# Attention on 64-token halves, with the running state carried twice per chunk, in a fused gated-linear-attention and MLP kernel

## The chip, the cores and the metric

The kernel runs on one core of one Trainium2 chip. A core has five engines that run side by side, each with its own instruction queue: PE (TensorE, matrix products), DVE (VectorE), ACT (ScalarE), POOL (GpSimd) and SP (SyncE, which here only starts transfers). Data lies in HBM; transfers (DMAs) bring it to the on-chip memory SBUF; products land in a second memory, PSUM, which has eight banks. The metric is the device time in microseconds of one execution; lower is better. A profile is one more execution, recorded instruction by instruction; its span runs from the first to the last instruction.

## The reference

Gated linear attention comes first, for 4 batches, 8 heads, 768 tokens and 48 values per head. Its output, with the heads side by side (384 values per token), goes through a normalisation and a two-layer MLP, and is added to the MLP's result:

```python
for t in range(S):
    state = alpha[:, :, t, :, None] * state + k[:, :, t] (outer) v[:, :, t]
    y[:, :, t] = q[:, :, t] @ state
x  = y as (batch, token, 384)
xn = (x - mean) / sqrt(var + 1e-6) * g_ln
out = x + relu(xn @ w_ch1) @ w_ch2          # 384 -> 1536 -> 384
```

All of it is in float32; the two weight matrices arrive as float64 and are rounded on the chip.

## The kernel before

**Attention.** The 768 tokens are six chunks of 128 (`c`); with four batches (`b`) there are 24 blocks of attention, `attention(c, b)`. A block takes the logarithm of alpha, sums it along the chunk with a product with a triangular matrix (`lps`, L249), and takes two exponentials: `eq` (the product of the alphas up to each token) and `ek` (its inverse). Then q is scaled by `eq` and k by `ek`, and the recurrence turns into plain matrix products:

- both are transposed on PE (`tps`, L272) and copied to SBUF (`qkT`, L276 on ScalarE, L278 on VectorE);
- scores are k times q for each head (`aps`, L285). Heads lie in pairs `p`, of which head `i` sits on rows 0 to 47 or 64 to 111. `copy_predicated` (L289) writes what lies on or under the diagonal into a score tile `at`. There are two of these tiles in all, taken by turns; their other halves stay zero;
- outputs are scores times v (L307) plus q times the state at the start of the chunk (L302), added up in one PSUM tile `yps`. Chunk 0 has no state, so no L302;
- the state's update is k times v over the chunk (`sps`, L321), added to the state by VectorE (L326) and multiplied by the chunk's total gate by GpSimd (L331). The gate is the last row of `eq`, turned from a row into a column by two small transfers through HBM (`row`, L262, and `gate`, L294). The last chunk updates no state.

The output `x` is copied out of PSUM (L311), sent to HBM as `kept` for the final addition, normalised, and transposed (`xps`, L349) into `xT` for the MLP.

**The MLP.** In chunk 0 it is plain: `hidden` (L372, 36 products over 12 column blocks) and `project` (L384, 48 products). In the later chunks both layers use a scheme with fewer products and more additions: `hidden_product` (L612) and `product` (L455), with sums on VectorE (`combine_x`, `combine_hidden`) and GpSimd (`combine_first`, `combine_weights`, which rework the weights once). The weights come in 12 pieces of 768 KB, six of the first matrix and then six of the second. Three stage buffers hold pieces in flight. `round_weights` takes three operations on VectorE (L168, L170, L172), one on ScalarE (L174), and further ones on VectorE (L176 to L183).

**What sets the order.** Every part of the work is a Python generator that yields after each step, and the string `ORDER` says which generator takes its next step: a lower-case letter is a block of attention (a to x, in the order of chunk and batch), A to L a weight piece, M the MLP's products, N, S, X their sums, R the activations, O the fetching of `kept`. A letter whose generator has ended does nothing. Each engine gets its instructions in the order in which the steps issue them and keeps that order; a semaphore holds an instruction until its operands are there and its target is free. All input transfers go through SP's queue, at the start alpha, then k and q, then v for the four batches, then three weight pieces. `attention` loads the alpha, k and q of a later block at its sixth step and the v of the next chunk near its end. The pool `ps` has two PSUM banks under the tag `s` (outputs, state update, `xps`), three under `a` (prefix sums, transposes, scores) and three under `m` (MLP).

Of the kernel before, what the change touches and what calls it, by code (L numbers as in the profile page):

```python
# [9 lines left out]
FP32 = mybir.dt.float32  # L10
# [15 lines left out]
    "babdabcdcabadcbacabbdabaabacababdabacbdbccbadAccdddcBcCedfeacbacaeBeffcgbaededbe"  # L26
    "eghfbAefgfcachfbdcheaaffbaefgdjBddeedbdcgfbeicCjgdfihcgjdCeAhccAgBDfghddEfeOgegi"
    "DfDeeiMfhMMMiMDMMiegMGEgEMMMOfeGghhigMMjhiCEfggFMhOGFHFgMGghMiHkfMMfiHeFIjhfHeMM"
    "IkJSIhhkhhlMMjIMfMglKJKjJLfgMljjLKLhhMSSMihSikMhOSgiMMSSMgShjkSjhiiMXjiSXSiXiXMk"
    "kMXkSllMXMXMlSMMXnMnMMkSMSMSiXmMSXMnMSMSMSMSjkMMkikjMXlMMMMMMRMllMMMljOMRSMMMSlk"  # L30
    "jlklMjjSRimMMnMSMjRMMMnMMMMkMnnmnMMMkMRMpjMMMnMRlMlllnmMmiRmOlMSmMRmMoMmmOMMJMRM"
    "SmSjmNSjlRMMRmoNinjkkNMmNMMkolMNRpoMlOKpMNMmMMMoMmoNmMNkNMMMNMMNMnMNqMkMNMMMopMM"
    "NSMMnolMoMlNpkNMoMMMOkOMMonnXXXXpMMXXMMXXXpoMMMMMMMMpXMMXMMoMMMrMMMMqMMMrMMMmnMM"
    "pRMomRnprmmMRqRopMMpMRMoMMmRmMMMMMrprnMnrnMMMoopppnMtpMqRMMMOMtrqMqnMMoMpqMprMRq"
    "RMMqNsMqMOMNRMNtrRnrMNMqMqqNMssRMMMNssoMMMNMNNMNsMMMNopMqqqqqrMMNMMsNtpMMNMMOprM"
    "MMNqsMqtMMooMMsNpMMXMMsMXXMstMqrrXtuXXXMtMMXXMMvMMMMXsvMMMtXMstMOrMMMMMMMMMvMMrr"
    "rsMtMvOsMMrtMMMMLuRMsMMvvMMMMMRRMtMrRMuMORvxMMMRRMstrMMstRqttsMqRuMsMMNRMuMRNMMN"
    "NMvMtuurvMxMMMMNsNtRtMMwNNvMMMsrMNMwMMNNMNMMwtNMMuMMuuMMMMMNuMwMNMMNwMMuttsxMMuv"
    "XXXvxMvuuXXXXxvwxMXMxxMMuwMXMwxMMXMMXMMMMMvMMwMwMxMMMRMuOwMuOMMwMMMMwuMMxwMwRMRM"
    "MxRMMRMvMMMMwxMMMMMMMMMuMMuMRMRRvMMMRNwxuRMMvMOMRxMMxvwMMNwMxNNMNxRNMMuxMMwMNMvM"  # L40
    "MONMwMNNMNMMMNwMMNMxMxMMvMMxwNMONMMNxMMMvMMXvOXXXMXXXMMMMMMXXMMMMMMMMXMMMMMRMXMM"
    "RMMMMMMMMMMMMMMMRRMMMMORMMMMMRMMMMRMMMMMMMMMRMRRMRMMNMMMNMMMNNNRMMNNMNMNMMMNNMMM"
    "ONMNMMMMMMMMMMMMMNNMMNMMMMMMM"
# [4 lines left out]
def kernel(  # L48
# [59 lines left out]

    r = np.arange(P)
    upto = (r[None, :] >= r[:, None]).astype(np.float32)  # L110
# [4 lines left out]
    def load(c, b, names="akqv"):  # L115
        for n, src in (("a", alpha), ("k", k), ("q", q), ("v", v)):
            if n not in names:
                continue
            t = raw.tile([P, H, D], FP32, name=f"r{n}", tag=f"r{n}",
                         bufs=B)  # L120
            nc.sync.dma_start(t, src[b, c * P:(c + 1) * P])
            raws[n, c, b] = t

# [88 lines left out]
    sts = [cpool.tile([P, NP, 2, D], FP32, name=f"st{b}") for b in range(B)]  # L212
    for b in range(B):
        nc.vector.memset(eqs[b].rearrange("p a b c -> p (a b) c")[:, :, D:], 0.0)
        nc.vector.memset(qks[b].rearrange("p i a b c -> p (i a b) c")[:, :, D:], 0.0)
        nc.gpsimd.memset(sts[b], 0.0)

# [7 lines left out]
    def eq_of(c, b):  # L225
        return eqs[b if c < 2 else b % 2]

    def qk_of(c, b):
        return qks[b if c < 2 else b % 3]


    ats = [cpool.tile([P, 2, NP, P], FP32, name=f"at{i}") for i in range(2)]
# [9 lines left out]
    def attention(c, b):  # L242
# [16 lines left out]
        if c + 1 < NCB:  # L259
            row = dram.tile([1, NP, P], FP32, name="row", tag="row")  # L260
            gate = work.tile([P, NP], FP32, name="gate", tag="gate", bufs=B)
            nc.sync.dma_start(row, eq_of(c, b)[P - 1:P].rearrange("o a b c -> o a (b c)"))  # L262
# [5 lines left out]
        qkT = work.tile([R, 2, NP, P], FP32, name="qkT", tag="qkT", bufs=2)  # L268
        for i in range(2):
            tps = ps.tile([R, NP, P], FP32, name="tps", tag="a", bufs=3)  # L270
            for p in range(NP):
                nc.tensor.transpose(  # L272
                    tps[:, p], qk_of(c, b)[:, i, p].rearrange("p a b -> p (a b)")[:, :R], ident)
            yield
            if i == 0 or c < 2:
                nc.scalar.copy(out=qkT[:, i], in_=tps)  # L276
            else:
                nc.vector.tensor_copy(out=qkT[:, i], in_=tps)  # L278
            yield
        at = ats[b % len(ats)]  # L280
        aps = [ps.tile([P, NP, P], FP32, name=f"aps{i}", tag="a", bufs=3) for i in range(2)]
        for p in range(NP):
            for i in range(2):
                rows = slice(64 * i, 64 * i + D)
                nc.tensor.matmul(aps[i][:, p], qkT[rows, 1, p], qkT[rows, 0, p],  # L285
                                 start=True, stop=True)
        yield
        for i in range(2):
            nc.vector.copy_predicated(out=at[:, i], data=aps[i],  # L289
                                      mask=mask.unsqueeze(1).broadcast_to([P, NP, P]))  # L290
        yield
        if c + 1 < NCB:
            with nc.allow_non_contiguous_dma(reason="one row to columns"):
                nc.sync.dma_start(gate, row.rearrange("o a c -> c (o a)"))  # L294
        yield
        vt = raws.pop(("v", c, b))
        yps = ps.tile([P, NP, 2, D], FP32, name="yps", tag="s")
        sides = [slice(64 * s, 64 * s + 64) for s in range(2)]
        for p in range(NP):
            if c > 0:  # L300
                for s in sides:
                    nc.tensor.matmul(yps[s, p].rearrange("p a b -> p (a b)"), qkT[:, 0, p, s],  # L302
                                     sts[b][:R, p].rearrange("p a b -> p (a b)"),
                                     start=True, stop=False)
            for i in range(2):
                for s in sides:
                    nc.tensor.matmul(yps[s, p, i], at[:, i, p, s], vt[:, 2 * p + i],  # L307
                                     start=(c == 0), stop=(c == 0 or i == 1))
# [6 lines left out]
        yield  # L315
        if c + 1 < NCB:
            sps = ps.tile([R, NP, D], FP32, name="sps", tag="s")
            heads = list(enumerate((slice(0, 64), slice(64, R))))
            for p in range(NP):
                for i, s in heads:  # L320
                    nc.tensor.matmul(sps[s, p], qk_of(c, b)[:, 1, p, i, :s.stop - s.start],  # L321
                                     vt[:, 2 * p + i], start=True, stop=True)
        yield
        if c + 1 < NCB:
            for i, s in heads:
                nc.vector.tensor_add(sts[b][s, :, i], sps[s], sts[b][s, :, i])  # L326
        yield
        if c + 1 < NCB:
            load(c + 1, b, "v")
            st = sts[b].rearrange("p a b d -> p a (b d)")  # L330
            nc.gpsimd.tensor_mul(st, st, gate.unsqueeze(2).broadcast_to([P, NP, 2 * D]))  # L331
# [393 lines left out]
```

## Time and profile before

| What | Value |
|---|---|
| Median of three runs | 476.33 us (474.06 to 476.4) |
| Span of the profiled execution | 472.3 us |
| PE busy | 457.1 us (97% of the span), 3,690 records |
| VectorE, ScalarE, GpSimd busy | 356.6, 152.9, 222.7 us |
| Outputs: scores x v (L307), q x state (L302) | 768 and 320 records, 36.5 and 29.8 us busy |
| Scores (L285) | 384 records, 28.6 us busy |
| Bytes moved | 43.29 MB in 40,132 packets |

The page gives the span of the profiled execution and no separate time for it; the median of the runs is 4.0 us above that span, which stands for what lies around it. A float32 product shows as two PE records. Busy times of PE count a record from its start to its end, and records overlap, so the distance of successive starts says more about a product's price than its length. "Idle before" names what ended a wait.

### The profile page before, as it was taken

What the parts mean: (1) busy time and instruction counts of PE and PEld (TensorE: products, weight loads), DVE (VectorE), ACT (ScalarE), POOL (GpSimd) and SP (SyncE); (2) the same over time, 40 slices, a digit from 0 to 9 for tenths busy, and PEclk for the clock granted to TensorE, in tenths of its full rate; (3) what the DMA queues carried; (4) which work ended last, traced back from release to release, by engine and by line L of the source; (5) the groups of instructions that cost most, each with busy time, mean ns of one, the idle gap of its engine ahead of it and who ended that gap; (6) DMA issues with size and microseconds to landing.
All of it is one profiled execution on the core that took longest, in us unless ns stands there. A gap on an engine that the chain in (4) does not pass through costs nothing.

```text
span 472.3 us, 9365 instructions
## 1 busy us (share of the span) xinstructions
PE 457.1 (97%) x3690; PEld 384.5 (81%) x3690; DVE 356.6 (76%) x662; ACT 152.9 (32%) x335; POOL 222.7 (47%) x222
## 2 busy tenths in 40 slices
PE   7899999999999999999999999999999999998996
PEld 5768465567688889998898998898998899987896
DVE  3799899867377799876788867688677579765673
ACT  4576354511033523124342121543031341223300
POOL 4142103069969990727461426460435360544513
PEclk9999999999999999999999999999999999999999
DMA  8986856403301422240331231330020110210001
GB/s 260 334 248 196 282 157 224 123 19 102 85 17 52 129 75 67 70 118 15 104 101 52 86 102 51 83 101 1 34 81 23 35 35 0 80 56 0 1 18 51
DMA packets 40132, 43.29 MB, mean 92 GB/s; under 512 B 13956, under 2 KB 36228, under 8 KB 40088
## 3 DMA queue, kind: packets, MB, share of 16 engines
q1 hardware_dynamic: 39544, 42.56, 29.4%
q8 instruction: 29, 0.48, 0.4%
q10 hardware_dynamic: 544, 0.13, 0.1%
q14 instruction: 15, 0.12, 0.1%
HBM read 33.20 MB, written 9.48 MB: 90 GB/s over the span
## 4 chain that ended last, share of the span: by engine, by line
PE 85%; DVE 5%; POOL 4%; ACT 2%; DMA 2%; issue 2%; POOLq 0%; DVEq 0%; ACTq 0%
PE ops L455 24%; PE hps L612 24%; PE hps L372 7%; PE ops L384 7%; PE aps L285 5%; PE yps L307 4%; PE tps L272 4%; PE yps L302 4%; PE lps L249 3%; PE sps L321 2%; PE xps L349 2%; DMA rk<-in_k_dram 1%; DVE at L289 1%; DVE sum L588 1%; DMA ra<-in_alpha_dram 1%
## 5 line engine op out<-in xcount | busy, mean ns | idle before, releaser
L471 POOL TENSOR_TENSOR ob<-ob,u 128x192 f32<-128x192 f32 x40 | 27.5, 699 | 83.3 <-DVE ob L468 63.9
L612 PE MATMUL hps<-sum,w 128*128 128x256 f32 x240 | 59.9, 382 | 1.1 <-DVE hT L655 1.1
L612 PEld LDWEIGHTS hps<-sum,w 128*128 128x128 f32 x240 | 44.7, 190 | 7.9 <-DVE hT L655 1.5
L455 PE MATMUL ops<-w,hT 128*128 128x192 f32 x280 | 49.6, 328 | 0.0
L664 ACT ACTIVATE hT<-hT 128x512 f32<-128x512 f32 x60 | 36.3, 628 | 35.6 <-POOL hT L634 21.3
L455 PEld LDWEIGHTS ops<-w,hT 128*128 128x128 f32 x280 | 45.7, 190 | 1.1
L331 POOL TENSOR_TENSOR st<-st,gate 128x384 f32<-128x384 f32 x20 | 19.1, 959 | 53.6 <-DVE st L326 44.3
L631 POOL TENSOR_TENSOR hT<-hT,u 128x512 f32<-128x512 f32 x10 | 12.9, 1287 | 56.9 <-DVE u L630 56.9
L256 POOL TENSOR_TENSOR qk<-rk,ek 128x384 f32<-128x384 f32 x22 | 23.3, 1059 | 30.0 <-PE sps L321 12.6
L307 PE MATMUL yps<-rv,at 128*64 128x48 f32 x768 | 36.5, 219 | 0.1
L289 DVE COPY_PREDICATED at<-consts,aps 128x512 f32<-128x512 int32 x48 | 32.2, 724 | 3.6 <-PE aps L285 3.2
L307 PEld LDWEIGHTS yps<-rv,at 128*64 128x64 f32 x768 | 32.9, 138 | 0.6 <-DVE at L289 0.3
L372 PE MATMUL hps<-xT,w 128*128 128x512 f32 x72 | 32.4, 597 | 0.0
L384 PE MATMUL ops<-w,hT 128*128 128x384 f32 x96 | 32.2, 488 | 0.0
L612 PE MATMUL hps<-xT,w 128*128 128x256 f32 x120 | 31.1, 382 | 0.9 <-DVE hT L644 0.9
L285 PE MATMUL aps<-qkT 48*128 48x128 f32 x384 | 28.6, 285 | 2.1 <-DVE at L289 1.3
L285 PEld LDWEIGHTS aps<-qkT 48*128 48x128 f32 x384 | 23.8, 187 | 8.0 <-issue 4.0
L302 PE MATMUL yps<-st,qkT 112*64 112x96 f32 x320 | 29.8, 257 | 0.0
L455 PE MATMUL ops<-ws,sum 128*128 128x192 f32 x160 | 28.9, 328 | 0.7 <-DVE sum L442 0.7
L455 PE MATMUL ops<-ws,hT 128*128 128x192 f32 x160 | 29.5, 327 | 0.0
L276 ACT COPY qkT<-tps 112x512 f32<-112x512 f32 x32 | 18.2, 597 | 29.0 <-PE tps L272 25.7
L455 PEld LDWEIGHTS ops<-ws,sum 128*128 128x128 f32 x160 | 26.3, 190 | 1.4 <-DVE sum L442 1.0
(141 smaller groups left out, 1020.9 us busy)
## 6 DMA issues: line engine op xcount, KB each, us to landing
ws<-in_moe_w_ch_dram SPq DMA_DIRECT2D x12, 768.0 KB, 6.1
ra<-in_alpha_dram SPq DMA_DIRECT2D x24, 192.0 KB, 2.6
rk<-in_k_dram SPq DMA_DIRECT2D x24, 192.0 KB, 3.4
rq<-in_q_dram SPq DMA_DIRECT2D x24, 192.0 KB
rv<-in_v_dram SPq DMA_DIRECT2D x24, 192.0 KB, 2.8
kept<-x SPq DMA_DIRECT2D x24, 192.0 KB, 1.9
ob<-kept SPq DMA_DIRECT2D x24, 192.0 KB, 2.9
out_dram<-ob SPq DMA_DIRECT2D x19, 192.0 KB, 1.9
```

What stands on the lines that cost most here:

```text
L256: nc.gpsimd.tensor_mul(qk[:, 1, :, :D], raws.pop(("k", c, b)), ek)
L285: nc.tensor.matmul(aps[i][:, p], qkT[rows, 1, p], qkT[rows, 0, p], start=True, stop=True)
L289: nc.vector.copy_predicated(out=at[:, i], data=aps[i], mask=mask.unsqueeze(1).broadcast_to([P, NP, P]))
L302: nc.tensor.matmul(yps[s, p].rearrange("p a b -> p (a b)"), qkT[:, 0, p, s], sts[b][:R, p].rearrange("p a b -> p (a b)"), start=True, stop ...
L307: nc.tensor.matmul(yps[s, p, i], at[:, i, p, s], vt[:, 2 * p + i], start=(c == 0), stop=(c == 0 or i == 1))
L331: nc.gpsimd.tensor_mul(st, st, gate.unsqueeze(2).broadcast_to([P, NP, 2 * D]))
L372: nc.tensor.matmul(hps, w1[:, f, j * P:(j + 1) * P], xT_of[c][:, f], start=(f == 0), stop=(f == NF - 1))
L384: nc.tensor.matmul(ops_of[b], hT_of[c][:, j, b], w2[:, j], start=(j == 0), stop=(j == NJ - 1))
L455: nc.tensor.matmul(acc, lhs[:, j], rhs[:, j], start=(j == 0), stop=(j == NT - 1))
L471: getattr(nc.gpsimd, f"tensor_{op}")(x, x, y)
L612: nc.tensor.matmul(acc[:, i], w, b, start=True, stop=True)
L664: nc.scalar.activation(out=x, in_=x, func=AFT.Relu)
```

## The change

Each chunk of 128 tokens is now worked on as two halves of 64.

- The triangular matrix is cut into two blocks, so that the sums of logarithms start anew at token 64, and `eq` and `ek` refer to the start of the half. There are two gates per chunk (two rows of `eq`, two columns), also in the last chunk.
- The transposed q is no longer in a tile of its own: it is copied straight into the score tile `at`, head 0 of a pair into rows 0 to 63 and head 1 into rows 64 to 111. The scores of a head go to the other half of the rows of the same tile. Scores are thus 16 products of 64x64 per block instead of 8 of 128x128, and each half's column of `at` holds q on some rows and scores on the others.
- v is loaded twice, in two layouts: `rv` has the rows that the state's update reads where v lies in its own half, and `va` has v in the rows that face the scores, while its other rows take the state. One product over all rows of `at` and `va` then gives scores x v plus q x state. A v load is six transfers of 64 rows with pieces of 48 values (192 bytes); it was one transfer with rows of 1,536 bytes.
- The state is updated after each half: `ups` holds two updates per chunk (one in the last), each is added by VectorE and multiplied by its gate by GpSimd, and after each a `carry` copies the state, head by head, into `va`: of this chunk for the second half, of the next chunk for its first half. Both copies of a carry are on ScalarE. Chunk 0 goes the same way, with a state that a memset has zeroed.
- All copies out of the transposes are on ScalarE (L298, L300 of the new kernel); the VectorE copy is gone.
- The state tile has half the width; `ORDER` is another string throughout.

The core of the diff, in which `HS` is 64 and `halves` are the two half ranges of 128 rows:

```diff
-    upto = (r[None, :] >= r[:, None]).astype(np.float32)
+    upto = ((r[None, :] >= r[:, None]) & (r[None, :] // HS == r[:, None] // HS)).astype(np.float32)
...
+            rv = raw.tile([P, NP, D], FP32, name="rv", tag="rv", bufs=B)
+            va = raw.tile([P, 2, NP, 2, D], FP32, name="va", tag="va", bufs=B)
+            src = v[b, c * P:(c + 1) * P].rearrange("(s t) (p i) d -> i s t p d", s=2, i=2)
+            for i in range(2):
+                nc.sync.dma_start(rv[halves[i]], src[i, i])
+                for s in range(2):
+                    nc.sync.dma_start(va[halves[1 - i], s, :, i], src[i, s])
...
-    ats = [cpool.tile([P, 2, NP, P], FP32, name=f"at{i}") for i in range(2)]
+    ats = [cpool.tile([P, NP, 2, 2, HS], FP32, name=f"at{i}") for i in range(2)]
...
-            if i == 0 or c < 2:
-                nc.scalar.copy(out=qkT[:, i], in_=tps)
+            if i == 0:
+                for j in range(2):
+                    nc.scalar.copy(out=at[rows[j], :, j], in_=tv[rows[j]])
             else:
-                nc.vector.tensor_copy(out=qkT[:, i], in_=tps)
+                nc.scalar.copy(out=kT, in_=tv)
...
+        for p in range(NP):
+            for s in range(2):
+                for i in range(2):
+                    rs = slice(64 * i, 64 * i + D)
+                    nc.tensor.matmul(aps[i][halves[1 - i], p, s], kT[rs, p, s], at[rs, p, i, s],
+                                     start=True, stop=True)
...
+        for p in range(NP):
+            for s, up in enumerate(ups):
+                for i, h in enumerate(heads):
+                    vs = rv[halves[s], p] if s == i else va[halves[s], s, p, i]
+                    nc.tensor.matmul(up[h, p], qk_of(c, b)[halves[s], 1, p, i, :h.stop - h.start],
+                                     vs, start=True, stop=True)
...
+        def carry(s, to):
+            for i, h in enumerate(heads):
+                nc.scalar.copy(out=to[h, s, :, i], in_=st[h])
+
+        for s, up in enumerate(ups):
+            nc.vector.tensor_add(st, up, st)
+            yield
+            nc.gpsimd.tensor_mul(st, st, gate[:R, s].unsqueeze(2).broadcast_to([R, NP, D]))
+            yield
+            if s == 0:
+                carry(1, va)
+                yield
...
         for p in range(NP):
             for i in range(2):
-                rows = slice(64 * i, 64 * i + D)
...
+                rs = slice(0, P if i == 0 else R)
+                for s in range(2):
+                    nc.tensor.matmul(yps[halves[s], p, i], at[rs, p, i, s], va[rs, s, p, i],
+                                     start=True, stop=True)
+        yield
+        if not last:
+            load(c + 1, b, "v")
+        yield
+        if not last:
+            carry(0, raws["v", c + 1, b][1])
```

## The prediction, made before the changed kernel ran

> **What bounds the kernel now.** I read the page's first part, then the busy times by stretch, then the start: its DMA queue, its VectorE and its PE timelines.
>
> ```profile
> span 472.3 us, 9365 instructions
> PE 457.1 (97%) x3690; PEld 384.5 (81%) x3690; DVE 356.6 (76%) x662; ACT 152.9 (32%) x335; POOL 222.7 (47%) x222
> ...
> PE 85%; DVE 5%; POOL 4%; ACT 2%; DMA 2%; issue 2%; POOLq 0%; DVEq 0%; ACTq 0%
> ```
>
> PE is busy 97% of the span and carries 85% of the chain that ended last: what PE has to do, and when it can begin, is the time. The stretches (busy us of each engine) say where it does not:
>
> ```profile
> 0.00:20.00 20.00, 15.22 (x143) 12.01 (x144) 9.94 (x21) 8.25 (x17) 8.07 (x15) 1.00 0.91 305
> 20.00:40.00 20.00, 18.29 (x269) 14.06 (x268) 18.79 (x38) 14.70 (x34) 6.58 (x7) 1.00 0.78 219
> 60.00:80.00 20.00, 20.00 (x145) 11.05 (x143) 19.36 (x32) 9.21 (x17) 4.72 (x5) 1.00 0.55 172
> ```
>
> PE's idle time is in the first 40 us (8.5 of some 15 us in all). From 20 to 40 us ScalarE (fourth number) is the fullest that it ever is, VectorE (third) is nearly full from 20 to 100, and the DMA share is 0.91 and 0.78. So the start is a chain of several engines, and everything after it is PE. The queue on SP at the start (start, us, what):
>
> ```profile
> 7.49 1.85 SPq L121 DMA_DIRECT2D rv<-in_v_dram  x4
> 9.58 1.88 SPq L156 DMA_DIRECT2D ws<-in_moe_w_ch_dram  x3
> ...
> 13.34 0.59 SPq L121 DMA_DIRECT2D rq<-in_q_dram  x1
> 16.11 0.33 SPq L121 DMA_DIRECT2D ra<-in_alpha_dram  x1
> 18.17 0.33 SPq L121 DMA_DIRECT2D rk<-in_k_dram  x1
> 20.21 0.33 SPq L121 DMA_DIRECT2D rq<-in_q_dram  x1
> ```
>
> An issue costs 0.46 us of the queue (1.85/4). In the built program each load waits for the load eight places ahead to have landed; the starts at 16.11, 18.17 and 20.21 are that wait for the three weight pieces, which so landed at 16, 18 and 20 us. VectorE begins to round the first piece at 18.3 and needs 2.43 us for the three operations:
>
> ```profile
> 18.30 0.94 DVE L168 TENSOR_SCALAR w<-ws 128x768 int32<-128x768 int32 x1
> 19.27 0.96 DVE L170 SCALAR_TENSOR_TENSOR w<-ws,w 128x768 f32<-128x768 uint32 x1
> 20.26 0.56 DVE L172 TENSOR_SCALAR ws<-ws 128x768 int32<-128x768 int32 x1
> 20.73 0.94 DVE L168 TENSOR_SCALAR w<-ws 128x768 int32<-128x768 int32 x1
> ```
>
> Last, PE where attention runs without a gap; successive starts give the price of each block:
>
> ```profile
> 44.78 0.35 PE L302 MATMUL yps<-st,qkT 112*64 112x96 f32 x4
> 44.97 0.39 PE L307 MATMUL yps<-rv,at 128*64 128x48 f32 x8
> 45.19 0.35 PE L302 MATMUL yps<-st,qkT 112*64 112x96 f32 x4
> 45.37 0.39 PE L307 MATMUL yps<-rv,at 128*64 128x48 f32 x8
> 45.59 0.63 PE L321 MATMUL sps<-rv,qk 128*64 128x48 f32 x16
> 46.15 1.16 PE L285 MATMUL aps<-qkT 48*128 48x128 f32 x16
> 47.24 1.12 PE L372 MATMUL hps<-xT,w 128*128 128x512 f32 x2
> ```
>
> A float32 matmul is two records. Outputs with the state cost 4 x (0.19 + 0.22) = 1.64 us, the update of the state 0.56, the scores 1.09. Single starts in the trace alternate: 6 and 105 ns in the scores, 6 and 40 to 52 ns where 48 columns meet 64 columns of weights. So a matmul's second record waits for its first, and the next matmul, on another part of the array, starts beside that second record. The price is one pass plus 6 ns per matmul, whatever the number of free parts.
>
> **What the Trainium skill says.** "TensorE: Matmul & The Clock Gate", Part 3, has matmuls on different tiles of the array overlap but start in order: the 6 ns agree. Its section LDWEIGHTS prices a weight load at columns/1.2 ns: 107 for 128 columns, 53 for 64, close to the 105 and 52 here, so 64 columns of weights set the pass whether 48 or 64 columns stream. The same page, Part 1 (engine queue depths), says that ScalarE and VectorE are strictly first in, first out; every order in this trace agrees, and the argument rests on it. "DMA: Bandwidth & Descriptors", Specifications, wants pieces of 512 B for line rate; the new v loads move 192 B pieces, and no run here shows such a piece.
>
> **The change part by part. PE after the change.**
> - Scores: 16 matmuls of 64x64 instead of 8 of 128 columns: 16 x (53+6 ns) = 0.95, plus the 0.15 to 0.2 that a block of scores has over its matmuls now (1.09 - 8 x 0.111): 1.1 us, as before. 24 times: 0.
> - State update: 16 matmuls (8 in the last chunk) instead of 8: 16 x 0.055 + 0.1 = 1.0 instead of 0.56; 20 x 0.44, and 4 x 0.56 where there was none: +11 us.
> - Outputs: 16 matmuls, 0.22 x 4 + 0.07 = 0.95, instead of 1.64: 20 x -0.69 = -14 us.
> Sum -3 us. Bounds: if four free parts let the update run at half its price, -13; if changing between tile shapes costs 0.1 us more per block, +4.
>
> **Other engines.** ScalarE: per block of attention two copies of q and one of k (0.60 each, the qkT copy's row) instead of one or two, and four small carries of some 0.3 (the 128x192 copies): +1.8 us in the first two chunks, where both were already on it. VectorE: 16 copies of 0.68 go (-11 us), all after chunk 1. GpSimd: 44 products of half size, 0.65 estimated from 0.96, instead of 20: +9 us. All three have room after 100 us (ScalarE 6 to 17 of 40), none in the start.
>
> **The queue and the start, followed through the order that was built.** Each v load is six issues instead of one: 24 issues instead of 4 ahead of the weights. From 7.5 us, with the wait for eight places ahead until the last q has landed (some 11 us), then 16 x 0.43: the weights are issued at 18.2 to 19, not 9.6, and land at 22.2, 24.3, 26.3 (2.05 us each as now), not 16 to 20. Behind them on SP: rows and gates (the first gate waits for weight piece 2 by the eight-places rule: issued 24.4, there at 27.5) and the loads of chunk 1.
> What is late next. In the new order ScalarE has two weight steps ahead of the first logarithm of chunk 1; they wait for VectorE's rounding of pieces 1 and 2. VectorE: 22.3 + 2.43, 24.7 + 2.3 = 27.0; ScalarE 27.1 + 1.0 = 28.1, logarithm to 28.6, PE's first prefix matmul of chunk 1 at 28.8, where it is 25.4 now. PE's list before it (two score blocks, one update) is over at some 19.4: PE idles 9 us.
> Then the outputs of batch 0: they wait for update, add, gate product, carry, as the state now comes in as rows of the second operand even in chunk 0. From 28 us ScalarE has, until x of the last batch: 5 logarithms (2.6), 8 exponentials (3.9), one weight step (1.0), 8 q and 3 k copies (6.6), 16 carries (4.8), 4 x (1.9), 2 rstd pairs (1.0): 21.9 us, in one queue with waits for PE (the two score tiles also hold q and are free only after the outputs). I get some 3 us of such waits, so 53; then norm, transpose, copy, 2.5: the first hidden product can start at 55.5, against 47.2 now. Bounds: 52 with no wait at all; 58 if 192 B pieces are slow (0.64 us a load) or PE's clock falls back in the gap: the first filler matmuls took 0.21 us per record where warm transposes of the same size take 0.11.
>
> **The sum.** I count what either PE list holds from the first hidden product on, at the prices above and 0.86, 0.65, 0.43, 0.33 us for the four product kinds (two issue distances each): 408.6 us before, 409 after, since the new order leaves about as much attention behind that point. Before, 472.3 - 47.2 - 408.6 = 16.5 us of small waits and tail; I keep them, as nothing in this order removes them. After: 55.5 + 409 + 16.5 = 481. Before's median 476.33 is 4.0 above the span: 485.
> VectorE's last rounding, which held the projections (PE reaches the last third at 101.4, VectorE ends at 97.8), has the same sum of work up to there (82 and 81 us) and a later start; it ends near 106, while PE needs it at 111. It is covered by the same delay; if PE started earlier, it would bind near 104.
>
> **The rivals.**
> - The state's round trip stalls PE in every chunk: update, add, product, carry, add, product, carry is some 4 us with hand-overs, more behind GpSimd's 1.3 us operations. For it: 24 such trips. Against: PE's new order has 4 to 10 us of products between update and outputs. If 20 of them wait 0.5 us: +10, 495.
> - Faster: the start is no longer than now. For it: PE is short of other work only there, and the list up to the first hidden product is some 4 us shorter. It needs the first hidden product by 47 us; then -3 us of PE gives about 473. The point that decides is 50 us. Against: two engines in strict order behind weights that are issued 9 us later.
> - Half of the delay returns, for instance because later waits, 16.5 us now, shrink when other engines have run ahead: 477, no difference.
> - The change does not do what it says: PE's work does not fall, as the doubled update eats the gain. This I hold for nearly true; it is in the sum.
>
> **How the numbers follow.** My case (480 to 491) 0.58; round trips 0.14; no difference 0.13; faster 0.15. Half a per cent is about what a measurement of this kernel can tell. Range 474 to 494: it takes in the start at 52 to 58 (481.5 to 487.5) with PE's -13 to +4, and part of the round trips and of the faster case. Faster 0.15, same 0.13, slower 0.72.
>
> **What would show it.** The first hidden product at 53 to 58 us; weights issued near 18 us; a PE gap of 7 to 10 us before 30 us; ScalarE over 90% busy from 28 to 53; 4,138 PE records (3,690 + 384 scores - 320 state products + 384 updates); update 1.0, scores 1.1, outputs 0.95 us per block; the time from the first hidden product to the end within 5 us of the 425 now. Wrong would be a first hidden product before 50 us, or update blocks of 0.6.

## The result, and the profile after

The kernel after takes 516.08 us (median of four, 514.23 to 516.55), the kernel before 476.37 beside it: a ratio of 1.0833, 95% interval 1.0802 to 1.0863, 40 us slower. The profiled execution of after has a span of 514.5 us. The page's first part and chain:

```profile
span 514.5 us, 10644 instructions
PE 459.2 (89%) x4138; PEld 379.2 (74%) x4138; DVE 365.2 (71%) x650; ACT 208.6 (41%) x463; POOL 236.5 (46%) x254
...
PE 62%; DVE 15%; DMA 6%; SPq 5%; POOL 4%; ACT 4%; issue 3%; POOLq 0%; DVEq 0%
```

PE's busy time is what it was (459.2 for 457.1 us). Its idle time is not: 55.3 us for 15.2. In the sum, the loss is PE standing still; the equal busy times hide less work and slower matmuls, as shown below. PE's share of the chain fell from 85 to 62%; VectorE, transfers and SP's queue took its place. The stretches say when (same columns as before: PE, weight loads, VectorE, ScalarE, GpSimd, granted clock, DMA share, GB/s):

```profile
0.00:20.00 20.00, 12.51 (x74) 9.22 (x74) 6.13 (x16) 9.64 (x19) 8.73 (x23) 0.91 0.63 168
20.00:40.00 20.00, 6.54 (x116) 4.49 (x118) 12.39 (x19) 6.48 (x12) 1.62 (x3) 0.66 0.81 235
60.00:80.00 20.00, 14.57 (x101) 8.61 (x100) 14.30 (x26) 9.33 (x21) 1.46 (x2) 0.85 0.67 167
```

From 20 to 40 us no computing engine is even two thirds busy: each waits for another. PE is still a quarter idle from 60 to 80, where it was full. Places in PE's order, read from the trace (us at which the first record of each kind starts):

| | before | after |
|---|---|---|
| first hidden product (chunk 0) | 47.2 | 65.8 |
| first projection of chunk 0 | 89.0 | 114.4 |
| first product of chunk 1 | 126.9 | 167.2 |
| from there to the span's end | 345.4 | 347.3 |

So 18.6 us are lost up to the first hidden product, another 21.7 up to the first product of chunk 1, and 1.9 in the remaining 347. SP's queue at the start, as shown of before:

```profile
7.19 0.67 SPq L136 DMA_DIRECT2D rv<-in_v_dram  x1
7.90 1.25 SPq L138 DMA_DIRECT2D va<-in_v_dram  x2
...
23.46 1.66 SPq L173 DMA_DIRECT2D ws<-in_moe_w_ch_dram  x3
...
32.10 0.39 SPq L317 DMA_DIRECT2D gate<-row  x1
```

A v issue costs 0.61 to 0.67 us; 24 of them, with hardly a wait between, put the weights at 23.5 us (9.6 before) and the first gate at 32.1 (21.2 before). VectorE begins to round at 28.09 (18.30 before). PE's wait in the start, and its blocks where they stand next to each other:

```profile
34.61 1.65 PE L268 MATMUL lps<-la,consts 128*128 128x384 f32 x2 [12.68 <-ACT la L265]
...
39.64 1.14 PE L349 MATMUL yps<-va,at 128*64 128x48 f32 x32 [0.45 <-DVE st L337]
40.71 0.65 PE L292 MATMUL tps<-consts,more 128*112 128x128 f32 x4
...
46.82 1.15 PE L307 MATMUL aps<-at,kT 48*64 48x64 f32 x32
47.90 1.87 PE L268 MATMUL lps<-la,consts 128*128 128x384 f32 x4
...
81.87 0.25 PE L327 MATMUL ups<-rv,qk 64*64 64x48 f32 x1
...
82.48 0.70 PE L403 MATMUL hps<-xT,w 128*128 128x512 f32 x1
```

PE waits 12.7 us for the first logarithm of chunk 1. Outputs cost 1.07 us (40.71 - 39.64; 1.64 before), scores 1.08, the doubled update 0.61 (82.48 - 81.87; 0.56 before, for half as many matmuls). So PE's work did fall, by some 8 us as an estimate: 20 x 0.57 = 11 us in the outputs, less 20 x 0.05 in the updates and less four new updates of some 0.5 us in the last chunk. None of it shows in the busy time, because the matmuls lasted longer: in the run without the state's trip, below, the same 4,138 records are busy for 448.7 us at a mean granted clock of 0.984; in after they take 459.2 us at 0.966.

Last, pieces of the chain of after between the v issues and the first hidden product (start, us, what):

```profile
46.35 2.23 DMA gate<-row
...
52.09 2.52 DMA gate<-row
54.74 0.52 POOL st L339
...
57.35 2.35 DVE w L200 x3
```

The chain runs through the state's trip (gate transfer, gate product, carry, add), and through rounding that stands between the trip's steps in VectorE's queue.

### The profile page after: what moved, and what is told of

It reads as the page before. It is cut to its first block, busy times and chain, and to the rows that moved or that the text cites. A ratio compares the mean times of both kernels' runs of the same rounds, so it can differ in the third digit from the quotient of the medians.

```text
span 514.5 us, 10644 instructions
## 1 busy us (share of the span) xinstructions
PE 459.2 (89%) x4138; PEld 379.2 (74%) x4138; DVE 365.2 (71%) x650; ACT 208.6 (41%) x463; POOL 236.5 (46%) x254
## 4 chain that ended last, share of the span: by engine, by line
PE 62%; DVE 15%; DMA 6%; SPq 5%; POOL 4%; ACT 4%; issue 3%; POOLq 0%; DVEq 0%
PE hps L643 22%; PE ops L486 22%; PE yps L349 3%; PE ops L415 3%; SPq L138 3%; PE aps L307 3%; PE tps L292 3%; DMA gate<-row 2%; PE lps L268 2%; DVE w L187 2%; DVE ws L193 2%; PE ups L327 2%; DVE w L185 2%; DVE w L196 2%; DMA ws<-in_moe_w_ch_dram 2%
## 5 line engine op out<-in xcount | busy, mean ns | idle before, releaser
L339 POOL TENSOR_TENSOR st<-st,gate 112x192 f32<-112x192 f32 x44 | 30.5, 697 | 125.3 <-DVE st L337 69.6
L334 ACT COPY va<-st 64x192 f32<-64x192 f32 x88 | 30.7, 349 | 54.8 <-POOL st L339 45.1
L312 DVE COPY_PREDICATED at<-consts,aps 64x512 f32<-64x512 int32 x48 | 35.1, 732 | 15.0 <-PE aps L307 13.7
L268 PE MATMUL lps<-la,consts 128*128 128x384 f32 x48 | 23.4, 576 | 21.5 <-ACT la L265 21.4
L298 ACT COPY at<-tps 64x512 f32<-64x512 f32 (+1 forms) x48 | 27.8, 579 | 22.7 <-PE tps L292 22.1
L307 PEld LDWEIGHTS aps<-at,kT 48*64 48x64 f32 x768 | 24.9, 137 | 11.3 <-ACT kT L300 5.4
L307 PE MATMUL aps<-at,kT 48*64 48x64 f32 x768 | 28.3, 225 | 3.9 <-ACT kT L300 3.8
L349 PEld LDWEIGHTS yps<-va,at 128*64 128x64 f32 (+1 forms) x768 | 23.7, 137 | 8.1 <-DVE st L337 4.6
L292 PE MATMUL tps<-consts,qk 128*112 128x128 f32 x176 | 26.9, 288 | 3.0 <-DVE qk L277 1.6
L349 PE MATMUL yps<-va,at 128*64 128x48 f32 (+1 forms) x768 | 25.7, 223 | 4.0 <-DVE st L337 4.0
```

Of the source, the lines that this page charges most:

```text
L268: nc.tensor.matmul(lps[:, :DM], tri, la, start=True, stop=True)
L292: nc.tensor.transpose(tps[:, p], qk_of(c, b)[:, i, p].rearrange("p a b -> p (a b)")[:, :R], ident)
L307: nc.tensor.matmul(aps[i][halves[1 - i], p, s], kT[rs, p, s], at[rs, p, i, s], start=True, stop=True)
L312: nc.vector.copy_predicated(out=at[h, :, i], data=aps[i][h], mask=mask[h, h].unsqueeze(1).unsqueeze(1).broadcast_to([HS, NP, 2, HS]))
L334: nc.scalar.copy(out=to[h, s, :, i], in_=st[h])
L339: nc.gpsimd.tensor_mul(st, st, gate[:R, s].unsqueeze(2).broadcast_to([R, NP, D]))
```

## The experiments

Theories: A, the six v issues of a block hold up SP's queue. B, GpSimd's sums of weights run beside VectorE's rounding, and the two slow each other. C, the state's trip delays PE, by PE's own waits (C1) or by its operations on the other engines (C2). O, the new sequence is at fault. Where an edit builds on another, it says so. Ratios are to the kernel before in the same session; its medians lay between 474.0 and 476.4 us, so a difference of medians between two sessions is uncertain by some 2 us.

### A: the v issues

Weights ahead of v, in after:

```
-    for names in ("a", "kq", "v"):
+    for names in ("a", "kq"):
...
     for i in range(STAGED):
         load_weights(i)
+    for b in range(B):
+        load(0, b, "v")
```

> The kernel after, with one edit: the 24 issues of the first v loads stand behind the first three weight pieces in SP's queue instead of ahead of them. Nothing is left out. Theory A (the six v issues per block hold up SP's one queue, at the start and later): the weights are issued near 10 us instead of 23.5, VectorE rounds from about 16 us instead of 28.1, but 15 us of v issues now stand ahead of rows, gates and the loads of chunk 1, so only part of the 13 us returns: first hidden product at 55 to 60 us instead of 65.8, total 506 to 511. Theory B (VectorE and GpSimd slow each other from 116 to 165 us in the new order): the late part is unchanged, 510 to 516. Theory C (PE waits for update, add, gate product and carry): the same start gain, at most, 508 to 516.

Measured: 518.05 us, ratio 1.0909 (1.0857 to 1.0961), first hidden product at 68.7. Nothing is gained: the rounding begins at 23.0 instead of 28.1, behind the masking and the first add in VectorE's queue, but the first gates are issued at 34.2 and 36.2, 2 us later than in after.

Two issues of whole rows, in after (called V below):

```
-            rv = raw.tile([P, NP, D], FP32, name="rv", tag="rv", bufs=B)
...
-            for i in range(2):
-                nc.sync.dma_start(rv[halves[i]], src[i, i])
-                for s in range(2):
-                    nc.sync.dma_start(va[halves[1 - i], s, :, i], src[i, s])
+            for h in halves:
+                nc.sync.dma_start(va[h].rearrange("t s p i d -> t s (p i d)"), src)
...
+        carry(0, va)
         for s, up in enumerate(ups):
```

> The kernel after, with v loaded by two issues of 64 rows x 2 x 1,536 B per block instead of six of 64 x 4 x 192 B; a row then also fills the place of the state of the first half, so this carry moves from the end of the block before to after the update. Nothing is left out. Theory A: an issue stays near 0.5 us, so 4 us of queue per chunk instead of 15.7; weights issued near 12 us, first hidden product at 52 to 56 us, gates no longer 5 us late, total 483 to 495. Theory B: the start's 10 to 12 us return, the other 21 us of loss between the first hidden product and the first product of chunk 1 stay: 502 to 507. Theory C: as B, or worse since the carry now stands between update and add: 503 to 512.

Measured: 512.43 us, ratio 1.0779 (1.0734 to 1.0825).

```profile
7.33 5.28 SPq L135 DMA_DIRECT2D va<-in_v_dram  x8
12.65 1.89 SPq L170 DMA_DIRECT2D ws<-in_moe_w_ch_dram  x3
```

Weights are issued at 12.65, VectorE rounds from 21.5, and still the first hidden product starts at 64.0. A alone is refuted as the cause of the 40 us.

Both edits:

> The kernel after with both edits: v by two issues per block, and those of chunk 0 behind the first three weight pieces. Nothing is left out. Theory A: weights issued near 8 to 9 us, VectorE rounds from 15 us, first hidden product at 48 to 52 us, total 478 to 490. Theory B and C: the start's 14 to 17 us return and nothing else: 499 to 503.

Measured: 514.91 us, 1.0815 (1.0760 to 1.0869), first hidden product at 66.2. With v by two issues, too, weights ahead of v bring nothing.

The kernel before with six v issues (the core of the edit):

```
...
+                for i in range(2):
+                    nc.sync.dma_start(more_v[halves[i]], src[i, i])
+                    for h in range(2):
+                        nc.sync.dma_start(to[halves[h], :, i], src[i, h])
...
```

> The kernel before, whose v loads are each made of six issues of 64 x 4 x 192 B: four that fill the same tile, two that fill a tile that nothing reads. Nothing else is changed and nothing is left out. Theory A: 0.65 us an issue, 15.7 us of queue per chunk, weights issued near 23 us; the first hidden product moves from 47 to 60 to 66 us and the total from 476 to between 493 and 512. Theory B and C (the loss is of the new order or of the state's trip): the start's delay alone, as far as it isn't made up later: 480 to 492.

Measured: 498.25 us, 1.0485 (1.0436 to 1.0534), first hidden product at 61.2. SP's queue in it:

```profile
7.11 0.65 SPq L126 DMA_DIRECT2D rw<-in_v_dram  x1
7.80 1.25 SPq L128 DMA_DIRECT2D rv<-in_v_dram  x2
...
23.49 1.66 SPq L168 DMA_DIRECT2D ws<-in_moe_w_ch_dram  x3
```

The issues alone cost the kernel before 22 us, yet going from six to two in after returns 4 (and the intervals of after and of V, 1.0802 to 1.0863 and 1.0734 to 1.0825, overlap). Something as long lies beside the issues.

### O: the sequence

V in the old order, step by step (each letter of a batch in the old string stands for these steps of the new blocks):

```
masking    -> masking, gate, update, add, product, carry, add, product
outputs    -> outputs, x
transposes -> transposes of x, their copy
```

> The kernel after with v by two issues per block, and its steps put back into the order of the kernel before: each step of attention stands where the old order has its counterpart; the update, the two adds, gate products and carries follow the masking of the scores at once; x follows the outputs, and the transposed x its transposes, at once. Nothing is left out. Theory O (the sequence that was searched anew makes the start serial: in it ScalarE has two weight steps ahead of the logarithms of chunk 1, and few products stand beside attention): first hidden product at 46 to 54 us, first product of chunk 1 at 127 to 138, total 472 to 488. Theory C (the state's trip itself costs it, in any order): PE waits at every block, first hidden product after 58 us, total 500 or more. Theory B (VectorE and GpSimd slow each other): in the old order the rounding is over before the sums begin, so as O.

Measured: 562.04 us, 1.1807 (1.1737 to 1.1877), first hidden product at 84.7. One thing changes here in what is computed: the tile with the queries of chunk 2's last batch is written again before its outputs are formed, so these take another block's queries, at the same work. O is refuted in this form: set out in this way, the old sequence is 50 us slower than the new one.

V with the logarithms of chunk 1 ahead of the weight steps (the stretch of the string that changes):

```
-bbbbaaABAdaBAeecacfeCCafdfAdbb
+bbbbaaefeeffABAdaBAcacCCadAdbb
```

> The kernel after with v by two issues per block, and six letters of its order moved: logarithm, prefix product and exponentials of the first two batches of chunk 1 stand ahead of the first weight steps instead of behind them. Nothing is left out. Against 512.4 us with v by two issues alone. Theory O: PE's gap of 7.8 us before 28 us closes, the prefix products run near 20 us, first hidden product at 55 to 59 us instead of 64.0, total 503 to 508. Theory C: the outputs of chunk 0 still wait for add, gate product and carry, which are behind the rounding on VectorE: first hidden product at 61 to 64 us, total 509 to 513. Theory B: no change after 64 us, so at most the start's gain.

Measured: 515.30 us, 1.0849 (1.0805 to 1.0893), first hidden product at 67.0. PE's gap shrinks from 7.8 to 4.9 us, and a wait of 5.7 us for an add comes behind it.

V with the weights' sums on GpSimd behind the rounding, as in the last part of B, and the start rearranged (`W` issues a weight piece):

```
-bbbbaaABAdaBAeecacfeCCafdfAdbbbbaaabdC
+bbbbWWWaadaeecacfeafdfdbbbbaaabABABACCAdC
```

> The kernel after with v by two issues per block and the sums behind the rounding, and in the start the first weight pieces issued behind the first two gates and eight weight steps behind the first trips of batches 0 and 1. Nothing is left out. Against the same kernel without the new start (expected at 492 to 500). Theory C with the start as its main place: the outputs of batches 0 and 1 near 26 us instead of 34 and 38, first hidden product at 53 to 59 us instead of 64, total 482 to 493. Theory O' (the start is as long as its sum of VectorE and ScalarE work behind the weights, whatever stands first): 62 to 66 us, no gain.

Measured: 509.13 us, 1.0722 (1.0636 to 1.0808), first hidden product at 65.3; with the late sums and without the new start it is 507.38. Three ways to set out the same start reach the first hidden product at 64.0, 67.0 and 65.3 us. Moving work about in it returned nothing.

### C: the state's trip

V without adds, gate products and carries:

```
-            nc.vector.tensor_add(st, up, st)
...
-            nc.gpsimd.tensor_mul(st, st, gate[:R, s].unsqueeze(2).broadcast_to([R, NP, D]))
...
-                nc.scalar.copy(out=to[h, s, :, i], in_=st[h])
+            pass
```

> The kernel after with v by two issues per block, without the state's trip: the adds, the gate products and the carries are left out (44 + 44 + 96 operations), so that the outputs take v in the state's place and wait for v and the masked scores alone; the update products and the gate transfers still run. Against 512.4 us. Theory C: PE's waits for the trip are the loss: first hidden product at 48 to 54 us, total 475 to 492. Theory O: ScalarE gets some 11 us of work less before the first hidden product and PE some waits less, but the weight steps stay ahead of the logarithms: first hidden product at 55 to 60 us, first product of chunk 1 at 148 to 156, total 497 to 508. Theory B: 505 to 510.

Measured: 482.21 us, 1.0162 (1.0102 to 1.0222); first hidden product at 52.5, first product of chunk 1 at 137.8. Of the 36 us that V loses to before, 30 go with the trip: in the profiled executions 11.5 us up to the first hidden product, 10.4 from there to chunk 1 and 9.1 behind it. The 6 to 8 us that are left were not taken apart. Its page:

```profile
PE 448.7 (94%) x4138; PEld 372.8 (78%) x4138; DVE 347.2 (73%) x606; ACT 177.2 (37%) x375; POOL 211.6 (44%) x202
```

With all 4,138 PE records in it, PE is busy 448.7 us, 8 less than before: the gain that the blocks promised.

Then the trip was taken apart, always in V. Outputs that do not wait for it:

```
-        carry(0, va)
+        carry(0, spare_va)
...
-                carry(1, va)
+                carry(1, spare_va)
```

> The kernel after with v by two issues per block, whose carries write the state to a tile that nothing reads: the outputs take v in the state's place and wait for nothing of the trip, while every add, gate product and carry still runs. What is left out is the state's part in the outputs. Against 512.4 us with the trip and 482.2 us with its operations left out altogether. Theory C1 (PE waits for the trip at the outputs): 480 to 490. Theory C2 (the trip's operations fill ScalarE, GpSimd and VectorE, whose other work comes late behind them): 503 to 512. In between, both have their part, as the distance says.

Measured: 505.15 us, 1.0634 (1.0585 to 1.0684). PE's wait for the carries is worth 7 us of the 30, nearly all of it late: from the first product of chunk 1 to the end V takes 349.5 us and this run 343.1, while the first hidden product moves only from 64.0 to 63.3. But update and outputs share two buffers, which the adds must free. So, in addition, adds that take a fixed tile instead of the update:

```
-            nc.vector.tensor_add(st, up, st)
+            nc.vector.tensor_add(st, spare_va[:R, s, :, 0], st)
```

> The kernel after with v by two issues per block; carries write a tile that nothing reads, and the adds take a fixed tile in place of the update, so that the buffers that update and outputs share are free as soon as PE has filled them. Adds, gate products and carries all run; the state's part in the outputs and the update's in the state are left out. Against 505.2 us where only the outputs' wait for the carries is gone, and 482.2 us without the operations. Theory C1 (PE waits for the trip, at the outputs and at the buffers): 480 to 490, first hidden product near 53 us. Theory C2 (the work of the trip on ScalarE, GpSimd and VectorE): 499 to 506, first hidden product at 60 us or later.

Measured: 505.15 us, 1.0598 (1.0570 to 1.0626): the buffers cost nothing that can be told. C1 is worth some 7 us. The same add, with the carries back in `va`, so that the outputs wait:

> The kernel after with v by two issues per block; the adds take a fixed tile in place of the update, so that the shared buffers come free early, while the outputs still wait for the carries. The update's part in the state is left out. Against 512.4 us. If the buffers alone are the wait: 485 to 495. If the outputs' wait stands behind it: 506 to 513, since either of them holds PE at the same place.

Measured: 512.01 us, 1.0755 (1.0737 to 1.0774), as V.

No carries:

```
-                nc.scalar.copy(out=to[h, s, :, i], in_=st[h])
+            pass
```

> The kernel after with v by two issues per block, without the carries: ScalarE has 96 x 2 copies of 0.35 us less to do, the outputs take v in the state's place; adds and gate products run as before and still free the buffers. Against 505.2 us with carries that nothing reads. If ScalarE's work is the loss: 483 to 492. If it is the buffers or VectorE and GpSimd: 500 to 505.

Measured: 494.44 us, 1.0384 (1.0363 to 1.0406): ScalarE's copies, which nothing reads in the run at 505.15, cost 11 us.

All operations in their places, with no hand-over from one of them to the next (the add still waits for its update, the gate product for the gate's transfer):

```
-                nc.scalar.copy(out=to[h, s, :, i], in_=st[h])
+                nc.scalar.copy(out=carried[h, 0, :, i], in_=fixed[h])
...
-            nc.vector.tensor_add(st, up, st)
+            nc.vector.tensor_add(added, up, fixed)
```

> The kernel after with v by two issues per block; the trip's operations all run, of the same sizes and in the same places of their queues, but apart: the adds take the update and a fixed tile and write a tile of their own, the gate products work on the state alone, the carries copy the fixed tile to a tile that nothing reads. The recurrence is left out. Against 505.2 us with the hand-overs and 482.2 us without the operations. If the hand-overs among ScalarE, VectorE and GpSimd are the loss: 482 to 490, first hidden product at 53 to 57 us. If the work itself is: 500 to 505, first hidden product at 60 us or later.

Measured: 500.29 us, 1.0532 (1.0495 to 1.0569), first hidden product at 58.9, between the two places forecast for it. So the 30 us divide, taken away in this order: PE's waits 7.3 (512.4 to 505.15), hand-overs among the other engines 4.9 (to 500.3), the operations in their queues with the two waits that they keep 18.1 (to 482.2). C2 holds for the larger part. How much of the 18 is the operations' own time is not shown: in the first 64 us of this run GpSimd stands 30.7 us waiting for gates, with the rest of its queue behind it.

Carries on GpSimd instead of ScalarE:

```
-                nc.scalar.copy(out=to[h, s, :, i], in_=st[h])
+                nc.gpsimd.tensor_copy(out=to[h, s, :, i], in_=st[h])
```

> The kernel after with v by two issues per block, with the carries on GpSimd instead of ScalarE. Nothing is left out. Against 512.4 us. If hand-overs and ScalarE's queue are the loss: a carry follows its gate product on the same engine and ScalarE loses 192 copies, 496 to 506. If GpSimd's longer queue, with its sums, takes their place: 510 to 520.

Measured: 520.68 us, 1.0963 (1.0907 to 1.1018). First hidden product at 58.9 and first product of chunk 1 at 147.7, 5 and 12 us earlier than V; but from there to the span's end it takes 370.5 us where V takes 349.5. GpSimd's queue then holds both the MLP's sums and the outputs up: PE waits 7.4 us at the hidden products, for an operation of VectorE that itself waited 8.8 us for GpSimd, and 7.5 us for carries. Taken out at one place, the work is paid for at another.

No trip, but six issues for v:

```
-                nc.sync.dma_start(va[h].rearrange("t s p i d -> t s (p i d)"), src)
+                for i in range(2):
+                    nc.sync.dma_start(va[h, 0, :, i], v[b, c * P:c * P + HS].rearrange(
+                        "t (p i) d -> i t p d", i=2)[i])
+                nc.sync.dma_start(va[h, 1].rearrange("t p i d -> t (p i d)"), src[:, 1])
```

> The kernel after without the state's trip (adds, gate products and carries left out) and with v by six issues per block: four of 64 x 4 x 192 B and two of 64 x 1,536 B. Against 482.2 us with two issues. If the delays by v and by the trip lie beside each other in the kernel after, so that each hides the other: 494 to 504, as much as six issues cost the kernel before. If v's issues hardly cost in the new order: 482 to 488.

Measured: 507.97 us, 1.0660 (1.0640 to 1.0681). Without the trip the issues cost 25.8 us (24 by the two ratios), with it 3.6. The two delays lie beside each other, and each hides the other: that is why mending v alone returned so little.

### B: sums beside the rounding

VectorE and GpSimd in after, in the late part of the rounding. GpSimd's sums of weights run from 92.3 to 102.7 us and, after a wait for an add, from 116.4 on:

```profile
99.89 1.72 POOL L596 TENSOR_TENSOR rq<-rk,w 128x384 f32<-128x384 f32 x1
100.80 1.62 DVE L196 SCALAR_TENSOR_TENSOR w<-w,ws 128x768 f32<-128x768 f32 x1
...
108.58 0.96 DVE L196 SCALAR_TENSOR_TENSOR w<-w,ws 128x768 f32<-128x768 f32 x1
...
115.32 1.16 POOL L339 TENSOR_TENSOR st<-st,gate 112x192 f32<-112x192 f32 x1 [12.59 <-DVE st L337]
116.15 2.10 DVE L196 SCALAR_TENSOR_TENSOR w<-w,ws 128x768 f32<-128x768 f32 x1
...
132.20 2.04 DVE L196 SCALAR_TENSOR_TENSOR w<-w,ws 128x768 f32<-128x768 f32 x1
...
142.15 4.40 DVE L373 TENSOR_SCALAR xn<-x,mv,rstd 128x384 f32<-128x384 f32 x2 [0.60 <-ACT rstd L370]
...
173.18 1.49 DVE L312 COPY_PREDICATED at<-consts,aps 64x512 f32<-64x512 int32 x2 [1.24 <-PE aps L307]
```

The same operation takes 0.96 us while GpSimd stands still and up to twice as long beside its work. The masking, which reads scores from PSUM, keeps its 0.74 beside sums of the second matrix (at 173.18). V with the sums cut to eight columns (in both matrices, so that chunks 1 to 5 take unsummed weights; one of the two places is shown):

```
-                op(out[i], x[i], y[i])
+                op(out[i][:, :8], x[i][:, :8], y[i][:, :8])
```

> The kernel after with v by two issues per block, with GpSimd's sums of weights cut to 8 columns each, so that the products of chunks 1 to 5 take unsummed weights. Against 512.4 us. Theory B: VectorE's rounding operations keep 0.95 us from 110 to 160 us instead of 2 to 3.4, PE no longer waits 4.0 us for rounded weights, first product of chunk 1 at 145 to 152 us instead of 159.7, total 497 to 505. Theory O and C: first hidden product at 64 us as before, first product of chunk 1 at 156 to 160, total 508 to 513.

Measured: 492.00 us, 1.0352 (1.0304 to 1.0401). The same operations in it (its L193 is L196 of after):

```profile
116.81 1.00 DVE L193 SCALAR_TENSOR_TENSOR w<-w,ws 128x768 f32<-128x768 f32 x1
...
122.74 0.87 DVE L367 TENSOR_SCALAR xn<-x,mv,rstd 128x384 f32<-128x384 f32 x2 [0.60 <-ACT rstd L364]
```

From the first hidden product to chunk 1 it takes 81.9 us; V takes 95.7, before 79.7. The doubled times go with the sums, and 14 us of this stretch with them: B is shown. The Trainium skill, "SBUF — State Buffer", Who interferes with whom, says that an operation of VectorE with two inputs in SBUF, or in a two-port mode, contends with a GpSimd operation that reads SBUF, and that one of the two waits. The doubled times here agree, and GpSimd's sum lasts longer as well (1.72 us at 99.89, 0.99 for one of the same size at 93.99). In the kernel before, the last rounding ends at 97.8 us, and all but the first of the 17 sums for the first matrix come from 99.4 on.

V with the sums of the first matrix behind the rounding (the `S` letters that stand ahead of the last rounding letter are moved behind it, and this line makes the sums wait for the last rounded piece):

```
+        nc.gpsimd.tensor_add(extra[:, 0, :1], w2[:, NJ - 1, :1], w2[:, NJ - 1, :1])
```

> The kernel after with v by two issues per block; GpSimd's 17 sums of weights are moved behind the last rounding step in the order, and a one-column sum that reads the last rounded piece stands ahead of them, so that none runs beside the rounding. Nothing is left out. Against 512.4 us, and 492.0 us with the sums cut to 8 columns. Theory B (the sums beside the rounding make VectorE's operations last twice as long): rounding operations of 0.95 us, rounding over near 120 us instead of 132, first product of chunk 1 at 143 to 150 us instead of 159.7, total 492 to 500. Rival (the sums cost by being in GpSimd's queue ahead of gate products, whenever they run): no gain, 508 to 516.

Measured: 507.38 us, 1.0686 (1.0617 to 1.0756). Chunk 1 begins at 146.6 instead of 159.7, as B had it, but the total is near the rival's forecast. What happens behind 146.6:

```profile
154.63 0.50 POOL L335 TENSOR_TENSOR st<-st,gate 112x192 f32<-112x192 f32 x1
155.17 0.71 ACT L329 COPY va<-st 64x192 f32<-64x192 f32 x2 [10.32 <-POOL st L335]
156.33 0.57 ACT L668 COPY hT<-hps 128x512 f32<-128x512 f32 x1
156.95 2.07 PE L638 MATMUL hps<-xT,rk 128*128 128x256 f32 x4 [7.12 <-ACT hT L668]
```

A gate product stands behind the late sums in GpSimd's queue, a carry waits 10.3 us for it on ScalarE, a copy of chunk 1's products stands behind the carry, and PE waits 7.1 us for that copy. From its first product on chunk 1 takes 48.1 us to the second matrix where V takes 39.0. So the rival is true as well: in this kernel the sums cost either by what they run beside or by what stands behind them. The rounding ends at about 122 us and the sums of the first matrix need 26 after it; that much is no longer free.

Both edits, no trip and late sums:

> The kernel after with v by two issues per block, without adds, gate products and carries, and with the sums of weights behind the rounding. The state is left out. Against 482.2 us without the state and 492.0 without the sums. If the two losses are separate, 512.4 - 30.2 - 12 to 20: 462 to 470, first product of chunk 1 at 124 to 130 us. If they are one loss seen twice, 478 to 484.

Measured: 488.96 us, 1.0296 (1.0238 to 1.0354), 7 us slower than without the trip alone and outside both forecasts: PE waits 8.6 us at the hidden products for sums on VectorE that wait for GpSimd. So B's remedy adds nothing once the trip is gone. Whether the sums beside the rounding still cost anything there is not shown, as no run leaves out both.

No run is faster than the kernel before.

## Why the prediction was wrong

The sign was right and the place half right; the size was missed by 31 us, beyond the range.

- **PE after the change** (-3 us). The step "one pass plus 6 ns per matmul, whatever the number of free parts" failed. The update costs 0.61 us a block, not 1.0, which the prediction itself named as a sign of being wrong: with four free parts, twice the matmuls of before take hardly longer, near the half price that the prediction gave as its lower bound. Scores (1.08) held; outputs cost 1.07, not 0.95. PE's work fell by some 8 us. The error ran against the result. What was not in the sum is that matmuls last longer in an execution with more waits (459.2 us, at a mean granted clock of 0.966, for the records that take 448.7 at 0.984 without the trip): in after this took the 8 us back.
- **The queue.** The term 0.43 us per v issue was mis-sized; it measured 0.65. (The wait until some 11 us, put ahead of 16 of the issues, did not come; they ran from 7.2 us on.) Weights were issued at 23.5 us, not 18.2 to 19, and the rounding began at 28.1, not 22.3. The six-issue run puts the price of this mechanism in the kernel before at 22 us.
- **The start.** The list of what ScalarE does was near (26.5 us busy from 30.7 to 65.8; 21.9 forecast, with an earlier end), but "some 3 us of such waits" failed: it stood idle for 8.7 us there, and it began late. From 28 to 53 us it was busy 16.8 of 25 us, not over 90%. PE's gap lasted 12.7 us, not 9. The first hidden product came at 65.8, outside the bounds of 52 to 58. Also, the start is not a chain with the queue at its head: with the queue mended it is 64.0.
- **"Nothing in this order removes" or adds waits after it**: the step that failed most. I kept the 425 us from the first hidden product on; it took 448.7. The rounding, called covered and due near 106 us, ended at 138.4. It began late, the trip's operations stood in the same queue, and GpSimd's sums ran beside it and doubled its operations. I counted GpSimd's and ScalarE's added work as having room after 100 us because their busy shares were low; but what stood behind that work, or ran beside it, was late for PE. The runs give the trip's operations, with the waits that they keep, 18 of its 30 us, and the sums beside the rounding 14 us between the first hidden product and chunk 1.
- **The rivals.** The round trips (495 us) named the right object, and their mechanism is there at about its size: PE's own waits are worth 7 us, for the 10 forecast, and lie in chunks 1 to 5. The larger part of the trip's cost, in the queues of the other engines, they did not have. "Faster" and "half of the delay returns" fell; chunks 1 to 5 returned nothing (347.3 us for 345.4; 340.4 without the trip). "PE's work does not fall" fell too: it fell, and the end did not show it.

## What to carry to other kernels

A low busy share over the whole span is no room: price added operations on each in-order engine in the stretch where that engine's late result is what PE needs next, here the rounding of weights in the first 140 us. When a change adds several delays, take each out alone and all but one out: two that lie beside each other look harmless one at a time (3.6 us for the v issues in one kernel, 22 and 26 in two others). And before work is moved to an idle engine, or to a later place in its queue, see what it will run beside and what stands behind it there.

## What the runs showed of the hardware that was not expected

- An issue on SP's queue costs by its shape and not by its bytes: mostly 0.33 to 0.46 us for 128 rows of 1,536 B, and no more (0.38 in the median) for a weight piece of 768 KB; 0.61 to 0.67 for 64 x 4 pieces of 192 B, and 0.66 for 64 x 2 rows of 1,536 B (5.28 us for eight). On 64 rows, 256 short pieces were no dearer to issue than 128 long ones.
- On the DMA engines a 192 B piece took 17 ns and a 1,536 B piece 75 on average (36,864 and 17,792 packets in the trace of after): dearer per byte, by 1.8. No run separates this price from that of the issues.
- Four free parts of the array do run together: the 32 records of an update take 0.61 us where 16 took 0.56 before.
- Around PE's gap in the start, the granted clock was 0.66 (20 to 40 us). Right behind the gap the two records of a prefix product took 1.65 us (34.61), where before's took 0.91. The Trainium skill, "TensorE: Matmul & The Clock Gate", Part 1, has the clock halve after an idle window of 3.4 us; the durations, 1.8 times as long, agree in size.
- VectorE's rounding lasts up to twice as long beside GpSimd's sums (0.96 to 2.04 us for two float32 inputs of 128x768); two normalisations of 0.48 us took 4.4.
